# Products of zeros and of the identity ahead of 14 TensorE operations in a fused attention and gating kernel

## The chip, the cores and the metric

The kernel runs on one core of a Trainium2 chip. The metric is the device time of one execution in microseconds (us). Engines are named as in the profile: PE is TensorE's matmul stream and PEld its weight loads, DVE is VectorE, ACT is ScalarE, POOL is GpSimd, SP is SyncE.

## The reference

Two layers are computed one after the other. The first is linear attention with positive random features, for 8 batches, 8 heads, 576 positions and 64 channels; the second mixes along the sequence by a Fourier product and gates the result.

```python
def phi(x):                                    # x: q or k, scaled
    h = x @ omega.T - sum(x * x) / 2           # 128 features
    return exp(h - max(h)) / sqrt(128)
q_p, k_p = phi(q), phi(k)
num = q_p @ (k_p.T @ v)
den = q_p @ sum(k_p) + 1e-6
x = num / den                                  # heads side by side: (8, 576, 512)
x1, x2, x3 = split(x @ w_proj)
y = x1 * irfft(rfft(x2) * rfft(filter_fft)) * x3
out = y @ w_out
```

The kernel does the Fourier transforms as matmuls with tables of sines and cosines that it makes itself at the start.

## The kernel before

Each batch's 576 positions are four tiles of 128 and a rest of 64; the rests of two batches are joined. All matmul operands are bf16.

Per batch, attention does this. **Turns** of keys and queries (`turn_keys`, `turn_queries`, both through `transposes`): eight 128x128 matmuls with the identity `ident` turn a half of `kn` or `qn` into a PSUM bank `h`, and VectorE (ScalarE for later queries) copies it to `kt` or `qt`. **Scores** (`key_features`): eight matmuls of `kt` with the features `om2`, 64 rows each, into a pair of PSUM banks `a`, then one exponential on ScalarE to `ek`; four such units make a batch. There are two pairs `a` and four banks `h`, so a new unit waits until an earlier one has been read. **Values** (`weigh_values`, `max_to_c`): VectorE takes maxima over `ek` (`h<-ek` in the profile, then `mx`), inverts them and scales `vn` to `vc`. **Queries**: 512-column matmuls of `qt` and `om2`, exponential to `eqt`. **Sums**: `ek` times `vc` gives `kv`. **Turn out**: `eqt` times `kv`, divided by VectorE (`xb`), is turned to `xt`. The joined rests go through `left_keys` (`kl`, `klt`, `ekl`, `vcl`) and their own queries. The second layer then projects `xt` with `wproj` (`gates` and `project2`), transforms, multiplies and projects with `wout`.

At the start, VectorE and ScalarE make the tables: `make_residues`, `sines`, then `tables`, which turns them on TensorE into `fwb` and its kin. `half_table` fills `gz`: its upper 64 partitions are zeros, the lower ones a copy of a table.

The order of the work is written out by hand. The kernel's body only records operations: `Plan.record` makes one numbered operation of each call, and joins successive TensorE calls of one stage that write the same PSUM tile into one operation. `ORDER` lists the numbers, and `issue` (line 230, the line of every row in the profile) sends the operations to the engines in that order. Each engine works through its own part in order, and waits between engines follow from the data. Loads are issued from POOL's queue, stores and small moves from SP's.

In the stretch that the prediction speaks of, TensorE's queue runs: first query turns of batch 0, the turn of omega, the rest's key turns, the other query turns, the rest's key scores (`klt`), key turns of batch 0, turns of tables (`gtab`, `xf`), then key scores and key turns of batches 0 and 1 interleaved with queries of batch 0. VectorE copies `kt` four times there, once for each half of the keys of batches 0 and 1.

Of the kernel before, what the change touches and what calls it, by code (L numbers as in the profile page):

```python
# [20 lines left out]

P = 128

CROSSED = {"keys": 5, "queries": 5, "out": 5}

ORDER = """
599 29 33 31 34 56 30 9 0 32 57 3 5 4 38 27 39 28 6 2 40 35 50 49 7 51 52 45 46 55 53 11 12 23 47 41
42 43 71 99 24 48 72 138 8 85 97 44 70 1 26 54 74 73 16 18 13 86 25 87 10 88 37 76 586 64 98 588 589
36 65 100 67 69 58 66 68 600 89 59 90 91 590 75 60 62 61 143 149 92 63 140 93 112 114 150 152 154
155 587 145 14 22 21 111 591 113 151 153 161 101 108 110 156 94 102 107 109 103 104 105 157 163 162  # L30
159 95 106 164 139 158 160 165 96 115 116 126 127 211 120 181 121 128 182 123 229 122 124 125 117 20
144 172 223 118 119 174 175 177 166 230 167 176 135 178 133 593 224 171 247 134 136 131 129 225 173
130 132 227 596 168 169 170 17 19 214 595 603 602 604 179 180 615 617 248 195 196 197 616 146 618
192 193 194 147 231 233 15 78 611 613 249 213 189 217 623 597 250 592 598 190 186 191 625 594 187
188 258 260 624 83 221 286 626 200 201 202 204 203 137 183 185 184 226 321 612 198 205 206 609 199
734 614 228 207 601 661 322 208 610 232 673 662 262 660 81 212 235 236 80 289 670 736 209 290 234
632 251 264 735 257 605 210 259 148 215 77 218 606 674 671 252 667 216 672 237 291 295 668 296 238
293 675 607 292 253 261 347 627 142 737 254 350 676 628 141 255 669 256 294 679 680 284 222 738 687
663 82 348 220 79 263 298 297 740 664 608 665 299 688 629 300 726 677 678 728 239 240 241 242 244
630 243 245 246 265 266 631 666 305 685 686 641 642 643 267 275 633 648 649 650 689 647 652 655 651  # L40
645 276 277 693 694 705 278 691 692 706 634 636 635 656 657 707 653 708 644 709 637 279 306 280 281
282 654 639 646 268 269 307 308 309 270 681 658 659 323 682 310 283 324 365 325 271 366 272 219 303
739 359 304 367 369 371 372 360 319 301 320 741 695 362 342 619 273 690 727 302 700 696 343 697 364
621 373 344 274 823 361 822 729 374 722 723 363 316 724 480 311 620 730 699 701 318 474 725 313 745
315 312 732 747 710 684 683 349 622 345 638 640 702 698 703 746 375 731 749 748 317 314 704 346 713
714 758 326 355 329 742 733 330 743 353 288 287 351 331 760 893 840 895 368 385 370 824 744 386 829
841 711 712 337 451 452 327 376 377 378 328 720 338 750 842 751 719 752 334 335 379 830 285 332 383
384 333 425 476 354 897 848 899 849 356 357 894 755 339 336 394 756 432 757 477 358 434 340 715 896
753 825 387 721 754 905 716 341 832 844 845 388 717 826 827 907 419 481 396 828 428 781 782 783 759
898 900 718 430 762 393 862 833 389 863 856 857 771 917 761 773 390 395 919 831 391 768 769 784 838  # L50
770 839 786 772 427 397 84 843 774 763 775 764 765 767 776 766 381 846 399 847 429 785 834 835 777
778 852 853 431 398 433 836 850 837 851 400 392 380 483 352 787 382 800 801 401 402 788 435 789 790
794 403 404 906 405 908 486 882 411 436 876 489 412 795 877 858 859 491 802 437 438 413 791 780 921
878 879 860 855 864 865 861 406 493 922 803 495 779 439 854 881 407 793 408 440 883 804 414 415 866
416 818 918 488 479 424 923 819 490 475 924 453 454 417 920 870 867 869 871 455 418 874 884 909 911
426 880 891 890 449 820 805 409 821 796 872 450 446 410 469 797 496 448 798 925 868 497 873 470 471
927 885 792 926 928 932 886 892 441 498 443 934 499 887 472 799 910 912 806 888 945 423 422 875 807
947 492 473 442 444 1027 500 501 502 1092 901 903 1094 946 445 485 889 1009 447 902 948 949 904 503
1093 958 494 462 960 959 463 1095 459 942 943 482 961 944 929 930 1014 962 460 950 951 952 464 1015
537 808 1084 1086 931 815 933 465 816 809 810 811 817 1080 1082 505 954 953 466 467 935 484 420 421  # L60
478 936 461 1081 456 457 1012 1013 955 971 973 956 458 507 937 1083 938 468 543 544 957 963 939 545
1010 1011 940 1035 546 1036 913 812 1085 563 915 564 1087 540 539 972 914 984 1028 941 542 813 508
916 1029 1019 487 985 986 541 975 974 1031 509 1020 1032 1051 1104 1106 504 968 1018 510 511 512 513
964 519 521 1052 514 1016 1017 1033 516 969 970 1100 1102 1034 1021 515 518 1105 1101 517 1045 965
506 976 1030 520 1022 1046 522 523 1103 547 1023 548 549 1107 550 524 1025 530 977 978 525 979 980
526 538 1026 1096 1043 1044 1047 1098 1097 1037 1038 1024 1048 527 1049 1088 1090 1050 1099 528 529
531 533 1039 534 967 1005 1006 1112 535 814 1114 532 536 557 554 559 966 996 999 556 1000 1040 551
1053 1089 553 555 558 997 1065 560 1066 1054 1055 1057 1091 1056 1279 565 1113 566 1058 552 1059
1115 998 1042 1001 1041 1215 1061 561 1071 567 562 1069 574 575 576 1070 1063 577 578 1064 1068 1281
981 982 983 1072 990 1132 579 991 992 581 582 1271 1273 583 1060 1197 1280 571 584 1062 1282 1134  # L70
993 572 573 1275 994 585 1120 1277 1116 1117 1118 568 1119 1276 1121 1214 1196 1199 569 1007 1008
995 1272 1067 570 1278 1200 1133 1123 1222 1122 1274 1135 1124 1198 1125 1136 1002 1223 1201 580
1129 1203 1202 1003 1130 1204 1004 1131 1230 1108 987 1231 988 989 1126 1218 1205 1127 1206 1216
1219 1220 1221 1236 1237 1238 1232 1233 1110 1235 1234 1137 1128 1208 1239 1209 1078 1077 1079 1138
1073 1217 1224 1225 1139 1140 1074 1174 1175 1176 1076 1155 1159 1157 1075 1158 1160 1210 1211 1156
1171 1177 1178 1179 1207 1240 1241 1141 1162 1161 1163 1164 1244 1165 1109 1111 1167 1166 1172 1245
# [157 lines left out]
def kernel(  # L234
# [11 lines left out]
    nc = Plan(tc.nc, tc)  # L246
# [29 lines left out]
    def bank():  # L276
        return nc.tile(psum, [P, 512], FP32, name="h", bufs=4)

    def bank_t():
        return nc.tile(psum, [P, 512], FP32, name="h", bufs=4)  # L280
# [42 lines left out]
    ident = nc.tile(const, [P, P], BF16, name="ident")  # L323
# [48 lines left out]
    for j in range(2):  # L372
        nc.vector.tensor_scalar_mul(
            out=om2[j * D : (j + 1) * D, :], in0=omt[:D, :MF], scalar1=qk_scale
# [28 lines left out]
    gz = nc.tile(const, [P, EC], BF16, name="gz")  # L403
# [2 lines left out]
    hps = nc.tile(const, [P, 3, DM], BF16, name="hps")  # L406
    hqs = nc.tile(const, [P, 3, DM], BF16, name="hqs")
    lo64, hi64 = slice(0, 64), slice(64, 128)

    residues = {}  # L410

# [86 lines left out]
            )  # L498

    def half_table():  # L500
        nc.vector.memset(gz[hi64], 0.0)
        nc.vector.tensor_copy(out=gz[lo64], in_=gtab[lo64, 2, HC : HC + EC])
        nc.vector.memset(gtab[lo64, 2, HC : HC + EC], 0.0)

    def tables():
# [3 lines left out]
            out=dup[:, 0], in_=gta[:, SL // 2 : SL // 2 + SL].unsqueeze(1).to_broadcast([P, 2, SL])  # L509
        )  # L510
        nc.vector.tensor_copy(
            out=dup[:, 1:3], in_=gns[:, :, SL // 2 : SL // 2 + SL].unsqueeze(2).to_broadcast([P, 2, 2, SL])
# [4 lines left out]
        dupf = dup[:].rearrange("p c j s -> p c (j s)")  # L517

        ps = bank()
        pb = ps[:].bitcast(BF16).rearrange("p (g c) -> p g c", g=8)  # L520
        for g in range(8):
            m, kt_ = g // 3, g % 3
            nc.tensor.transpose(
                out=pb[:, g],
# [122 lines left out]
    xt_tiles = {}  # L647
    kv_tiles = {}

    def transposes(dst, srcs, scalar=False):  # L650

        ps = bank_t()
        pb = ps[:].bitcast(BF16).rearrange("p (g c) -> p g c", g=8)
        for g, src in enumerate(srcs):
            nc.tensor.transpose(out=pb[:, g, :], in_=src, identity=ident[:])
        if scalar:
            nc.scalar.copy(out=dst, in_=pb[:, 0 : len(srcs)])
        else:
            nc.vector.tensor_copy(out=dst, in_=pb[:, 0 : len(srcs)])
# [34 lines left out]
    def key_features(*units):  # L694

        made = []
        for ek_out, kts in units:
            ps = two_banks()
            made.append(ps)
            for g, kt in enumerate(kts):  # L700
                for j in range(2):
                    nc.tensor.matmul(
                        out=ps[:, j, g * MF : (g + 1) * MF],
                        lhsT=kt[rows[j]],
                        rhs=om2[rows[j]],
                        start=True,
                        stop=True,
                    )
        for ps, (ek_out, _) in zip(made, units):
            nc.scalar.activation(  # L710
                out=ek_out, in_=ps[:].rearrange("p j (g m) -> p j g m", m=MF), func=AF.Exp
            )
# [686 lines left out]
```

## Time and profile before

| | us |
|---|---|
| three executions | 257.41, 258.19, 259.14 |
| their median | 258.19 |
| profiled execution | 259.44 |
| its span in the profile | 257.4 |
| PE busy | 238.1 (92%) |
| DVE busy | 217.9 (85%) |
| ACT busy | 200.7 (78%) |
| POOL busy | 62.6 (24%) |

The profiled execution is one of its own. It is 2.0 us longer than its span, which counts from the first to the last instruction. Busy shares are means over the whole span, and the stages differ: what limits the first 40 us need not be what limits the rest, so views of single stretches are of more use here. In a row of the timeline the first number is the start, the second the duration of the group, then engine, line, operation, output and inputs, form and count; a bracket at the end gives the idle time of the engine just before and what ended it.

### The profile page before, as it was taken

The page shows a single profiled execution, that of the slowest core. Times are in us where ns is not written, and L with a number is a line of the kernel's source. Part 1 is how long each engine was busy: PE and PEld are TensorE (multiplying, and loading weights), DVE is VectorE, ACT ScalarE, POOL GpSimd, SP SyncE. Part 2 cuts the span into 40 slices and gives each one's busy share as a digit, 9 for nine tenths or more (in the row PEclk, how much of TensorE's full clock was granted, in tenths as well). Part 3 has the DMA queues.
Part 4 walks back from the last instruction along what each step waited for, and adds up shares of the span by engine and source line. Part 5 has one row for each costly group of instructions (what it writes and reads, how often), then busy time and mean ns, then how long its engine had stood idle before and what let it go on. Part 6 is the DMA issues. An engine that isn't in the chain of part 4 may idle for free.

```text
span 257.4 us, 5843 instructions
## 1 busy us (share of the span) xinstructions
PE 238.1 (92%) x2282; PEld 139.2 (54%) x2282; DVE 217.9 (85%) x494; ACT 200.7 (78%) x324; POOL 62.6 (24%) x87
## 2 busy tenths in 40 slices
PE   0688699999999999999999979999999999999993
PEld 0555565655667465545566635555555545556641
DVE  6879998589697989999999887999867899899970
ACT  4689398899999999996888847894786568757653
POOL 8456363784007209403037000000000000000000
PEclk9999999999999999999999999999999999999998
DMA  6999999999938999998999977431635524223166
GB/s 83 184 193 178 198 173 140 146 167 176 155 85 128 157 141 110 160 138 142 149 230 128 177 91 188 100 68 34 140 110 143 109 80 122 81 62 113 52 230 220
DMA packets 86787, 35.28 MB, mean 137 GB/s; under 512 B 58219, under 2 KB 81256, under 8 KB 86760
## 3 DMA queue, kind: packets, MB, share of 16 engines
q0 software_dynamic: 59616, 17.31, 65.0%
q1 hardware_dynamic: 27000, 17.47, 27.4%
q8 instruction: 18, 0.29, 0.5%
q10 hardware_dynamic: 144, 0.13, 0.2%
q14 instruction: 9, 0.07, 0.1%
HBM read 34.64 MB, written 9.44 MB: 171 GB/s over the span
## 4 chain that ended last, share of the span: by engine, by line
PE 71%; DVE 10%; DMA 9%; ACT 6%; issue 1%; POOL 1%; SPq 0%; ACTq 0%; DVEq 0%
PE h L230 59%; PE a L230 12%; DMA qn<-in_q_dram 4%; DMA out_dram<-osb 4%; ACT osb L230 2%; DMA sw<-sp 1%; DVE h L230 1%; DVE vc L230 1%; DVE xb L230 1%; DVE kt L230 1%; ACT x L230 1%; DVE xt L230 1%; DVE vcl L230 1%; DVE qt L230 1%; ACT yt L230 1%
## 5 line engine op out<-in xcount | busy, mean ns | idle before, releaser
L230 PE MATMUL h<-xt,wproj 128*128 128x512 bf16 x256 | 64.5, 379 | 1.6 <-ACT osb L230 1.6
L230 ACT CAST x<-h 128x512 bf16<-128x512 f32 x68 | 40.1, 606 | 13.3 <-PE h L230 12.9
L230 PEld LDWEIGHTS <-wproj 128*128 128x128 bf16 x384 | 31.1, 98 | 27.5 <-issue 3.7
L230 ACT ACTIVATE osb<-h 128x512 f32<-128x512 f32 (+4 forms) x49 | 27.2, 566 | 12.5 <-PE h L230 4.1
L230 ACT ACTIVATE eqt<-a 128x1024 bf16<-128x1024 f32 x32 | 32.6, 1048 | 3.4 <-PE a L230 3.1
L230 ACT ACTIVATE ek<-a 128x1024 bf16<-128x1024 f32 x32 | 33.1, 1050 | 1.7 <-PE a L230 1.6
L230 PE MATMUL h<-wproj,xf 128*128 128x512 bf16 x128 | 32.4, 379 | 0.0
L230 PE MATMUL h<-wout,yt 128*128 128x512 bf16 x128 | 31.4, 379 | 0.0
L230 POOL DMA_DIRECT2D qn<-in_q_dram x26 | 23.7, 918 | 20.3 <-DMA qt<-qn 12.6
L230 DVE TENSOR_TENSOR x<-h,x 128x512 bf16<-128x512 f32 x32 | 21.7, 685 | 5.2 <-PE h L230 4.3
L230 PEld LDWEIGHTS <-yt 128*128 128x128 bf16 x128 | 12.1, 98 | 13.8 <-DVE vc L230 0.4
L230 PEld LDWEIGHTS <-xf 128*128 128x128 bf16 x134 | 12.1, 98 | 12.7 <-issue 1.0
L230 PE MATMUL h<-x,fwb 128*128 128x512 bf16 x72 | 18.6, 379 | 0.0
L230 DVE TENSOR_TENSOR xb<-a,rden 128x512 bf16<-128x512 f32 x24 | 16.2, 684 | 0.4
L230 PEld LDWEIGHTS <-eqt 128*128 128x128 bf16 x256 | 11.7, 98 | 6.0 <-DVE xb L230 1.0
L230 PE MATMUL a<-om,kt 64*128 64x128 bf16 x256 | 13.2, 231 | 1.3 <-ACT eqt L230 0.5
L230 PE MATMUL a<-kv,eqt 128*128 128x65 bf16 x256 | 13.0, 194 | 1.5 <-DVE xb L230 0.8
L230 PE MATMUL h<-ident,qn 128*128 128x128 bf16 x80 | 7.2, 238 | 7.4 <-DMA qn<-in_q_dram 7.4
L230 ACT CAST sp<-h 128x512 bf16<-128x512 f32 x16 | 9.7, 603 | 5.6 <-PE h L230 5.5
L230 DVE RECIPROCAL rden<-a 128x8 f32<-128x8 f32 x36 | 7.1, 200 | 7.1 <-PE a L230 6.9
L230 PE MATMUL h<-gtab,xs 128*128 128x193 bf16 x64 | 13.0, 247 | 0.0
L230 PE MATMUL a<-qt,om 64*128 64x512 bf16 x64 | 11.6, 389 | 1.1 <-ACT ek L230 0.3
(164 smaller groups left out, 512.1 us busy)
## 6 DMA issues: line engine op xcount, KB each, us to landing
out_dram<-osb SPq DMA_DIRECT2D x24, 256.0 KB, 2.3
vn<-in_v_dram POOLq DMA_DIRECT2D x8, 512.0 KB, 8.3
kn<-in_k_dram POOLq DMA_DIRECT2D x7, 512.0 KB, 8.6
qn<-in_q_dram POOLq DMA_DIRECT2D x24, 128.0 KB, 8.2
sw<-sp SPq DMA_DIRECT2D x16, 128.0 KB, 2.4
wproj<-in_moe_w_proj_dram POOLq DMA_DIRECT2D x3, 512.0 KB, 8.2
qn<-in_q_dram POOLq DMA_DIRECT2D x2, 512.0 KB, 7.6
out_dram<-xf SPq DMA_DIRECT2D x4, 256.0 KB, 2.9
```

Source lines behind the costliest of these rows:

```text
L230: getattr(real, name)(*args, **kw)
```

## The change

A table `WARM` names, by stage and batch, how many products are put in front of successive operations. `warm` issues them into the PSUM tile that the operation is about to write, with `start=True` each, so that the operation's own first write replaces what they left. For the queries of batch 0 the operands are `gz`'s upper half, 64 rows of zeros by 193 columns, in front of the turn that stands first in TensorE's queue; elsewhere both are the identity, 128 rows by 128 columns. Eight more identity products stand in `tables`. The zeroing of `gz`'s upper half moves from `half_table` to where `gz` is made; it was and is the first instruction of VectorE. `ORDER` is renumbered for that and otherwise lists the same operations in the same order.

```diff
+WARM = {
+    ("turn", "turn queries", 0): [0, 28],
+    ("turn", "keys", 0): [4, 0],
+    ("score", "left keys", 0): [14],
+    ("score", "keys", 0): [4, 4, 4, 3],
+    ("turn", "keys", 1): [4, 4],
+    ("score", "keys", 1): [4, 4, 4, 4],
+}
...
+    nc.vector.memset(gz[hi64], 0.0)
...
     def half_table():
-        nc.vector.memset(gz[hi64], 0.0)
         nc.vector.tensor_copy(out=gz[lo64], in_=gtab[lo64, 2, HC : HC + EC])
...
         ps = bank()
+        for _ in range(8):
+            nc.tensor.matmul(out=ps[:, 0:P], lhsT=ident[:], rhs=ident[:], start=True, stop=True)
         pb = ps[:].bitcast(BF16).rearrange("p (g c) -> p g c", g=8)
...
+    warms = {k: list(v) for k, v in WARM.items()}
+
+    def warm(kind, ps):
+        counts = warms.get((kind, *nc.where))
+        if not counts:
+            return
+        n = counts.pop(0)
+        if kind == "turn" and nc.where[0] == "turn queries":
+            a, w = gz[hi64, 0:P], gz[hi64, :]
+        else:
+            a, w = ident[:], ident[:]
+        for _ in range(n):
+            nc.tensor.matmul(out=ps[:, 0 : w.shape[-1]], lhsT=a, rhs=w, start=True, stop=True)
+
     def transposes(dst, srcs, scalar=False):
 
         ps = bank_t()
+        warm("turn", ps)
...
             ps = two_banks()
             made.append(ps)
+            warm("score", ps[:, 0])
```

The lists are used up from the left in the order of the recorded program. Note two things: the counts follow the program and not `ORDER`, so within the scores of the keys of batch 0 the list reads first unit 4, second 4, third 4, fourth 3, while TensorE's queue takes the unit with 3 first; and the first turn of queries in the program has 0, the second, which is first in the queue, 28.

## The prediction

> **What bounds the kernel now.** I read four views, in this order: the page's engine rows, the windows by stage, the chain of waits in order of time, and the timelines of TensorE and VectorE over the first 37 us. The windows first:
>
> ```profile
> 12.90:21.60 8.70, 7.85 (x83) 5.30 (x84) 6.85 (x19) 7.60 (x9) 5.97 (x8) 1.00 1.51 193
> 21.60:37.00 15.40, 11.61 (x178) 8.26 (x178) 14.98 (x29) 11.28 (x15) 8.66 (x12) 1.00 1.69 182
> 37.00:257.40 220.40, 214.13 (x1986) 122.08 (x1985) 186.56 (x413) 174.65 (x291) 39.64 (x50) 1.00 0.85 132
> 252.70:256.10 3.40, 0.68 (x4) 0.10 (x1) 0.28 (x1) 0.98 (x2) 0.00 (x0) 1.00 0.94 324
> 256.20:257.40 1.20, 0.00 (x0) 0.00 (x0) 0.00 (x0) 0.00 (x0) 0.00 (x0) 0.50 0.00 0
> ```
>
> The columns are length, then busy time of PE, PEld, DVE, ACT, POOL, the clock, DMA. From 37 us on TensorE sets the pace (214 of 220 us, and the chain stays on it nearly throughout). From 21.6 to 37 us VectorE does: 14.98 of 15.40 us, and in that stretch it waits for no other engine. Before 13 us the chain runs through the tables on VectorE and ScalarE, which take nothing late from TensorE. Only between 13 and 21.6 us does VectorE wait for TensorE. The waits of VectorE in that window are one line, and its timeline shows the three places:
>
> ```profile
> DVE kt L230 <- PE h L230: 1.8, 3, 0.8
> ```
>
> ```profile
> 15.37 0.69 DVE L230 COPY kt<-h 128x1024 bf16<-128x1024 bf16 x1 [0.62 <-PE h L230]
> ...
> 18.60 0.69 DVE L230 COPY kt<-h 128x1024 bf16<-128x1024 bf16 x1 [0.82 <-PE h L230]
> 19.21 0.28 DVE L230 COPY xf<-gns 128x256 bf16<-128x256 bf16 x1
> 19.34 1.22 DVE L230 TENSOR_TENSOR h<-ek 128x2048 bf16<-128x2048 bf16 x1
> 20.87 0.69 DVE L230 COPY kt<-h 128x1024 bf16<-128x1024 bf16 x1 [0.31 <-PE h L230]
> ```
>
> So 1.76 us (0.62 + 0.82 + 0.31) is all that a faster TensorE can take out of the path. ScalarE sits beside it: its exponentials run almost without a break from 13.27 us, when its table is loaded, to 26.8 us, with 0.48 and 0.38 us lost to TensorE in this window.
>
> **The clock.** The page's clock digit is 9 from the first slice, because the trace records only changes: the first record is at 20.6 us. What stood before it is read from TensorE's own timeline:
>
> ```profile
> 7.20 1.03 PE L230 MATMUL h<-ident,qn 128*128 128x128 bf16 x8 [7.20 <-DMA qn<-in_q_dram]
> ...
> 13.00 0.29 PE L230 MATMUL h<-ident,xf 128*128 128x128 bf16 x1 [0.20 <-DVE mk L230]
> ...
> 18.50 0.61 PE L230 MATMUL a<-qt,om 64*128 64x512 bf16 x2
> ...
> 20.77 0.39 PE L230 MATMUL a<-qt,om 64*128 64x512 bf16 x2
> ...
> 21.59 0.40 PE L230 MATMUL a<-om,kt 64*128 64x128 bf16 x8
> 21.92 0.62 PE L230 MATMUL h<-ident,qn 128*128 128x128 bf16 x8
> 22.47 0.39 PE L230 MATMUL a<-qt,om 64*128 64x512 bf16 x2
> ```
>
> The same pair of 512-column products takes 0.61 us at 18.50 and 0.39 us at 20.77; eight turns take 1.03 us before and 0.62 us after. TensorE is at half clock until 20.6 us. One turn costs (1.03 - 0.29)/7 = 0.106 us at half clock; at full clock eight turns hold the next operation back 0.55 us (21.92 to 22.47) and eight scores 0.33 us (21.59 to 21.92), against 0.96 and 0.54 us before.
>
> [...]
>
> [...]
>
> **The change part by part.** All other engines keep their instructions and their order; TensorE gets 93 products.
> - **28 zero products before the first turn of queries.** Zeros are written on VectorE at 0.85 to 1.07 us, already first in its queue, so nothing is pushed back. By columns one takes 193/128 x 0.106 = 0.16 us, 28 take 4.5 us: from 1.1 to 5.6 us at half clock, and less if it opens on the way. The first turn waits for its data until 7.20 us. Cost nothing, with 1.6 us to spare. [...] No row shows zeros; from below they count as nothing (the clock then opens by about 10 to 14 us, from turns and fills), from above as any product; I take the latter, since the row nearest is any matmul of the same shape.
> - **Staying open.** Between 5.6 and 7.2 us TensorE is idle. [...]
> - **14 identity products before the scores of the left keys.** 14 x 0.057 = 0.8 us, laid from about 9.3 us; these scores wait for VectorE's om2 until 11.01. Nothing at full clock, 0.2 us at half.
> - **8 before the tables' turns and 3 before the first scores.** They lie before a wait for VectorE's xf (12.95) and kt (13.61 us). Nothing at full clock.
> - **The other 40,** four before each of ten operations, 0.23 us a time. Before the scores whose keys VectorE has yet to copy they lie in a wait; before the three turns of keys (one of batch 0, two of batch 1) and before the second and fourth scores of batch 0 they stand in the queue and delay.
>
> **The sum.** First scores from 13.75 us (kt sets it). Then 0.33 of scores, 0.23 of fills, 0.62 of turns: kt copied at 14.97 instead of 15.37. Second scores: 0.55 + 0.23 + 0.40 after 14.31, ScalarE at 15.53 instead of 15.91. Third and fourth exponentials follow at ScalarE's 0.92 us: 16.45 and 17.36, each 0.38 early. The fourth scores' fills wait for the bank that the second exponential frees at 16.6; then 0.23, 0.33, 0.23 and 0.62 to the end of the next turns: 18.01, kt at 18.05 instead of 18.60, 0.55 early. h<-ek follows at 18.79 (the fourth exponential is done at 18.4) and leaves VectorE at 19.93; the last turns: scores start at 18.79 behind kt, 0.33, 0.23, 0.62, end at 19.97; kt at 20.01 instead of 20.87. **0.86 us early.** From there VectorE is its own bound to 37 us: ScalarE's last exponential comes 0.6 us early, still ahead of its reader at 27.4 - 0.86; v of batch 0 landed at 19.5 us against a use at 25.1, q of batch 1 at 16.5 against 21.9, the projection weights for the gates at 34.6 against 39.6. So the start of TensorE's full stretch moves by the same 0.86 us, and its work beyond is unchanged, as the last fill lies before 25 us.
>
> The profiled execution took 259.44 us (span 257.4): 258.6 after. The median of the runs is 258.19, 1.25 us below it; taking 0.86 off that gives **257.3 us**.
>
> **Rivals.**
> - **The clock falls back, or opens late** (near 12 to 14 us): the first two steps are lost, fills at half clock take some of the rest; gain about 0.3 us, 257.9. [...]
> - **The runs shown opened earlier than the profiled one.** [...] For it: the profiled time is the longest of the four.
> - [...]
> - **Slower: fills that run at half clock.** If zeros and identity do not open the clock before 20 us, five groups of four lie on the path (one turn and two scores of batch 0, two turns of batch 1) at 0.43 us each, 2.2 us, and 14 and 8 add up to 0.6: 260.4 to 261.0. It decides if the clock is still at half beyond about 13 us. [...]
>
> **How the numbers follow.** Forecast 0.52, fall-back 0.12, earlier runs 0.14, the large gain 0.14, slower 0.08. The likeliest alone: 256.6 to 257.9. The range reaches to the large gain below and past the small ones above: 255.8 to 259.0. About 1% (2.6 us) is what a measurement of this kernel can tell from no change; the sum caps near 1.8 us, so faster by over 1% takes the large gain with its late phases, and some scatter: 0.2; slower by over 1% the cold fills at their worst: 0.07.
>
> **What would show it.** Right: zero products at 1.1 us, eight query turns at 7.2 us taking 0.62 us, a clock record between 3.5 and 7 us; VectorE's waits for PE h at kt between 13 and 21 us at 0.9 instead of 1.8 us; PE's full stretch from 36.4. Wrong: turns at 1.03 us beyond 10 us, a second clock record before 20 us, or VectorE waiting anew after 21 us.

## The result and the profile after

| | median, us | range of 20 runs |
|---|---|---|
| before | 258.69 | 257.41 to 259.64 |
| after | 256.79 | 256.17 to 258.82 |

The ratio on record is 0.9946, 95% interval 0.9927 to 0.9964, so 1.40 us less (0.93 to 1.89). It equals 256.79 over 258.19, the median of the three executions given before; the medians of this table lie 1.90 us apart. 256.79 us is inside the range of the forecast (255.8 to 259.0, with 257.3 as its number) and within 1% of no change; the 0.86 us of the sum lies just under the interval.

The profiled execution of the changed kernel took 258.82 us (span 256.9) and is the slowest of its twenty. Its TensorE waited for the load of the rest's keys (`kl`) until 9.75 us where a second execution turns them from 8.58 us, and that delayed what hangs on it. So I read two executions: this one for the clock, the second (the first run below, 256.11 us) for the sum. TensorE's timeline of the first, in pieces:

```profile
1.13 4.71 PE L239 MATMUL h<-gz 64*128 64x193 bf16 x28 [1.13 <-DVE gz L239]
7.24 1.04 PE L239 MATMUL h<-ident,qn 128*128 128x128 bf16 x8 [1.41 <-DMA qn<-in_q_dram]
9.75 0.58 PE L239 MATMUL h<-ident,kl 128*128 128x128 bf16 x4 [1.22 <-DMA kl<-in_k_dram]
...
10.98 1.70 PE L239 MATMUL a<-ident 128*128 128x128 bf16 x14
...
13.15 1.03 PE L239 MATMUL h<-ident,kn 128*128 128x128 bf16 x8
...
15.92 0.61 PE L239 MATMUL h<-ident,kn 128*128 128x128 bf16 x8
```

The zeros stand where they were meant to, at 1.13 us, and end at 5.8. The first turns still take 1.04 us, so **the zeros have not opened the clock**. The 14 identity products after the late `kl` hold the left keys' scores back, and the key turns of 13.15 still run at half clock; those of 15.92 take 0.61 us. The first clock record is at 14.43 us (20.61 before). The row of VectorE's waits between 12.9 and 21.6 us:

```profile
DVE kt L239 <- PE h L239: 2.6, 3, 1.2
```

In this execution they are longer than before's 1.8 us. The windows, columns as before:

```profile
36.00:256.90 220.90, 215.71 (x2007) 123.31 (x2004) 188.45 (x415) 176.34 (x294) 41.17 (x52) 1.00 0.87 133
```

TensorE is busy for 215.7 of the 220.9 us from 36 us to the end. VectorE's scaling `vc<-vn` of the second batch, which marks the start of that stretch, begins at 36.82 us, 0.8 us later than before's 36.00; and yet the execution is 0.6 us shorter. So two things had to be told apart: what the start gives, and what is gained beyond it.

### The profile page after: what moved, and what is told of

Same layout as the page of the kernel before. It is cut to its first block, busy times and chain, and to the rows that moved or that the text cites. A ratio compares the mean times of both kernels' runs of the same rounds, so it can differ in the third digit from the quotient of the medians.

```text
span 256.9 us, 6029 instructions
## 1 busy us (share of the span) xinstructions
PE 244.4 (95%) x2375; PEld 145.8 (57%) x2375; DVE 218.0 (85%) x494; ACT 200.7 (78%) x324; POOL 62.6 (24%) x87
## 4 chain that ended last, share of the span: by engine, by line
PE 76%; DVE 8%; DMA 7%; ACT 4%; SPq 1%; issue 1%; POOL 1%; ACTq 0%; POOLq 0%; DVEq 0%
PE h L239 63%; PE a L239 13%; DMA out_dram<-osb 4%; DMA kl<-in_k_dram 2%; ACT osb L239 2%; DVE h L239 2%; DMA sw<-sp 1%; DVE xb L239 1%; DVE vc L239 1%; SPq L239 1%; DVE kt L239 1%; DVE vcl L239 1%; ACT sp L239 1%; DVE mx L239 1%; DVE qt L239 0%
## 5 line engine op out<-in xcount | busy, mean ns | idle before, releaser
L239 PEld LDWEIGHTS <-yt 128*128 128x128 bf16 x128 | 12.1, 98 | 13.8 <-DVE vc L239 0.4
L239 PE MATMUL a<-om,kt 64*128 64x128 bf16 x256 | 12.2, 218 | 0.5 <-DVE xb L239 0.4
L239 PEld LDWEIGHTS <-fwb 128*128 128x128 bf16 x81 | 7.4, 98 | 7.7 <-issue 0.2
```

The source lines that it names most:

```text
L239: getattr(real, name)(*args, **kw)
```

## The experiments

In each heading the ratio is against the kernel before on the same chip, with its 95% interval. "Start" is the begin of the second batch's `vc<-vn` on VectorE; "after the start" is the span less that. A run has one profiled execution, and it need not be like the median one; where the two differ, the text says so.

### The changed kernel again: 0.9914 (0.9889 to 0.9940)

No edit. 256.28 us, against 258.55 before on this chip.

> The changed kernel itself, unedited, for a second execution in the profile. Theory A (the zero products do not open the clock; the 65 identity products do, at about 10.5 to 14.5 us): turns of queries at 7.2 us take 1.03 us, the first clock record lies between 10 and 15 us; with the loads of kl landed near 8.1 us as before, VectorE's waits for kt between 12.9 and 21.6 us are 0.9 to 1.4 us. Rival B (the zeros open the clock in most grids and the profiled execution was an exception): first clock record between 3.5 and 7 us, turns at 7.2 us 0.62 us. Time 256.8 us, ratio 0.993 to 0.996 by either.

"Grids" in rival B stands for executions that differ in when the clock opens (16.58 to 22.92 us in the profiles of kernels without fills).

Its rows of TensorE, of VectorE and of VectorE's waits:

```profile
7.37 1.04 PE L239 MATMUL h<-ident,qn 128*128 128x128 bf16 x8 [1.54 <-DMA qn<-in_q_dram]
...
9.84 1.20 PE L239 MATMUL a<-ident 128*128 128x128 bf16 x14
...
11.35 0.62 PE L239 MATMUL h<-ident,kn 128*128 128x128 bf16 x8
```

```profile
14.88 0.69 DVE L239 COPY kt<-h 128x1024 bf16<-128x1024 bf16 x1
...
18.03 0.69 DVE L239 COPY kt<-h 128x1024 bf16<-128x1024 bf16 x1 [0.75 <-PE h L239]
18.77 1.22 DVE L239 TENSOR_TENSOR h<-ek 128x2048 bf16<-128x2048 bf16 x1
19.99 0.69 DVE L239 COPY kt<-h 128x1024 bf16<-128x1024 bf16 x1
```

```profile
DVE kt L239 <- PE h L239: 0.7, 1, 0.7
```

The turns of 7.37 run at half clock here too. The clock opens at 10.35 us, inside the 14 fills (1.20 us instead of 1.70), and the key turns of 11.35 take 0.62 us. The copies `kt` start at 14.88, 18.03 and 19.99 us; the sum said 14.97, 18.05 and 20.01. One wait of 0.7 us is left of 1.8. The start is 35.12 us, **0.88 early where 0.86 was forecast**. After the start 219.0 us are left, against 221.4 in the profile of before: another 2.4 us, which the forecast did not have.

### Without the 28 zeros: 0.9916 (0.9888 to 0.9944)

```diff
-    ("turn", "turn queries", 0): [0, 28],
+    ("turn", "turn queries", 0): [0, 0],
```

> The 28 zero products are left out, the 65 identity products stay. A: the zeros did nothing, so the time is that of the changed kernel, 256.8 us, ratio 0.994 within 0.002, clock record between 10 and 15 us. B: the clock opens 4 to 7 us later than with zeros, the first scores and turns run slow, 257.4 us, ratio about 0.997.

256.16 us, beside 256.28 with them. The first clock record is at 11.59 us, the start again at 35.12. The zeros are worth nothing.

### The zeros alone: 0.9991 (0.9969 to 1.0013)

All lists but that of the queries are set to zeros, and the loop of 8 in `tables` to `range(0)`.

> Only the 28 zero products stay; the 65 identity products are left out. A: as the kernel before, ratio 0.998 to 1.001, clock record near 14 to 21 us. B: clock record between 3.5 and 7 us if it does not fall back, ratio 0.993 or better, as the identity products no longer stand in TensorE's queue.

258.51 us beside 258.55: the kernel before. TensorE's row with the zeros is the same to the digit, and the key turns that took 0.62 us in the run above are at half clock:

```profile
1.13 4.71 PE L239 MATMUL h<-gz 64*128 64x193 bf16 x28 [1.13 <-DVE gz L239]
...
11.56 1.03 PE L239 MATMUL h<-ident,kn 128*128 128x128 bf16 x8
```

```profile
DVE kt L239 <- PE h L239: 1.8, 3, 0.8
```

The first clock record is at 20.65 us. **The whole gain belongs to the 65 identity products**: 2.2 us between this run and the first, on one chip. Their two profiled executions lie 2.5 us apart: the start gives 0.91 of that (36.03 to 35.12) and what follows 1.6 (220.6 to 219.0).

### Whole numbers in place of the zeros: 0.9916 (0.9892 to 0.9940)

Are zeros too poor in data to count? 24 products on 128 rows of the table `si` take the place of the 28.

```diff
-    ("turn", "turn queries", 0): [0, 28],
+    ("turn", "turn queries", 0): [0, 24],
...
-            a, w = gz[hi64, 0:P], gz[hi64, :]
+            a, w = si[:, 0:64].bitcast(BF16), si[:, 100:196].bitcast(BF16)
```

> The 28 zero products are replaced by 24 products of the same length on 128 rows of the table of whole numbers that POOL makes at 2.5 to 2.9 us (data that is not zero), the identity products stay. [...] B (zeros count like any product): the same time as the changed kernel within 0.1%.

256.36 us, within 0.1% of the changed kernel, as B has it; the first clock record is at 12.23 us. Still it does not show that zeros count: these 24 products did not open the clock before 12.23 us either, though their data is not zero and fills 128 rows. `si` is ready later than `gz`; whether that is the reason was not shown.

### Zeros in place of the identity: 0.9931 (0.9907 to 0.9955)

```diff
-            a, w = ident[:], ident[:]
+            a, w = eql_buf[0][:, 0, 0, :], eql_buf[0][:, 0, 0, :]
```

`eql_buf` holds zeros on 128 rows at that time. The 8 in `tables` become 64-row zeros of `gz`.

> The 65 identity products become products of zeros in the same places (57 of 128 rows from a tile that is zero until 47 us, the 8 of the tables of 64 rows); the 28 zeros at the start stay. Theory A (only products of data that is not zero open the clock): the clock record comes no earlier than in the kernel before, near 14 to 21 us or later, and the products now stand in TensorE's queue at half clock: 0.4 us each time four stand on the path, so slower than before, 259 to 261 us, ratio 1.001 to 1.010. Rival B (any product counts, and the zeros at the start were lost only to their 64 rows): clock record at 10 to 14.5 us, 256.3 us, ratio 0.992.

256.80 us, 0.7% below before on its chip. TensorE:

```profile
9.99 1.70 PE L239 MATMUL a<-eql 128*128 128x128 bf16 x14
...
12.16 0.68 PE L239 MATMUL h<-ident,kn 128*128 128x128 bf16 x8
```

The 14 fills of zeros end at 11.7 us, the clock opens at 12.32, and the turns of 12.16 are the first that run mostly at full clock. Without any fill of 128 rows (the run before the last) it stayed at half until 20.65. So zeros count, and what set the 28 apart was not their data. They differ in two other things: they fill 64 rows of the array and not 128, and they stand earlier, before 5.9 us.

### Only the first 25 fills: 0.9959 (0.9929 to 0.9989)

14, 8 and 3 stay; the zeros and the other 40 go.

```diff
-    ("score", "keys", 0): [4, 4, 4, 3],
-    ("turn", "keys", 1): [4, 4],
-    ("score", "keys", 1): [4, 4, 4, 4],
+    ("score", "keys", 0): [0, 0, 0, 3],
+    ("turn", "keys", 1): [0, 0],
+    ("score", "keys", 1): [0, 0, 0, 0],
```

> Only the first 25 identity products stay (14 before the left keys' scores, 8 in the tables, 3 before the first scores); no zeros, none of the other 40. If those 25 open the clock and it stays open by the kernel's own work, the 40 were on the path for nothing: VectorE's third wait for kt shrinks from 0.75 to 0.3 us or less, time 0.3 to 0.45 us below the changed kernel: 255.9 us, ratio 0.990. [...]

VectorE has the `kt` copies without a bracket, so without a wait:

```profile
17.17 0.69 DVE L239 COPY kt<-h 128x1024 bf16<-128x1024 bf16 x1
...
19.13 0.68 DVE L239 COPY kt<-h 128x1024 bf16<-128x1024 bf16 x1
```

The start is 34.26 us, 1.74 early: the whole 1.76 us of the three waits. The 40 fills thus cost 0.86 us of start (34.26 against 35.12). But the time is 257.53 us where 255.9 was expected: worse than with them (256.28) and with more scatter (256.56 to 259.61). After the start 221.2 us are left, about as before the change. In the waits from 36 us to the end stands one that the first run does not have:

```profile
PE h L239 <- ACT osb L239: 2.0, 1, 2.0
```

A second thing stands in the record of the single executions. The mean granted clock is 0.993 or less in 4 of these 12; they took 258.98 us in the median, the other eight 257.21. The mean leaves out the time up to the first clock record (the profile of before has 0.997, with half clock until 20.6 us), so a low mean says that the clock was at half again later: by estimate 0.993 is 3.6 us at half clock, and in the profiles the end of the run accounts for 1.4 us at most. Such a mean is seen in 58 of 140 executions of the kernels without the 40 later fills (before among them), in 2 of the 6 with whole numbers, and in none of the 61 of the other kernels with all 65 fills. So the 40 go with a clock that stays open. No execution with such a mean was profiled; where its clock fell, and whether near the start, is not shown.

### Where the rest is: a store near 150 us

That wait is in the profile of before too: TensorE's timeline, then ScalarE's.

```profile
151.47 1.03 PE L230 MATMUL h<-xt,wproj 128*128 128x512 bf16 x4
...
154.12 1.02 PE L230 MATMUL h<-xt,wproj 128*128 128x512 bf16 x4 [1.63 <-ACT osb L230]
```

```profile
153.47 1.09 ACT L230 ACTIVATE osb<-h 128x512 f32<-128x512 f32 x2 [3.14 <-DMA out_dram<-osb]
```

TensorE waits 1.63 us for a bank that ScalarE empties into `osb`; ScalarE waits 3.14 us for a buffer `osb`, which a store issued at 144.28 us still holds 9 us later, as the chain of waits has it:

```profile
144.28 9.11 DMA out_dram<-osb
```

In the first run the two rows are

```profile
150.35 1.89 PE L239 MATMUL h<-xt,wproj 128*128 128x512 bf16 x8
```

```profile
150.55 0.60 ACT L239 ACTIVATE osb<-h 128x512 f32<-128x512 f32 x1 [0.81 <-PE h L239]
```

where the eight matmuls follow each other without a break and ScalarE waits for TensorE, not for the store. Just before it, from 133 to 139 us, POOL's queue issues loads of `q` of batches 6 and 7 and `v` of batch 7. The small load `vl` behind them took 13.8 us from issue to landing before, and 8.9 us in the first run:

```profile
DMA to landing us min/median/max: 13.8/13.8/13.8
```

```profile
DMA to landing us min/median/max: 8.9/8.9/8.9
```

What stands directly ahead of the store in SP's own queue is not one of these loads. From batch 5 on the kernel turns keys and queries by transposing moves (DMA transfers that transpose on the way), and one of them is issued 3.0 us before the store (1.6 us in the first run):

```profile
141.24 2.94 SPq L230 DMA_TRANSPOSE kt<-kn  x1
```

```profile
140.12 1.46 SPq L239 DMA_TRANSPOSE kt<-kn  x1
```

By the completion signals in the traces this move ends at 151.65 us before and at 148.52 in the first run, the store at 153.39 and 149.06. In all fourteen traces the store ends 0.5 to 1.8 us after the move. So the store comes in right behind a move that itself takes 10.4 and 8.4 us here.

Two readings were open. Either any gain at the start reaches this store and is carried or lost there; or something else about the kernel decides it. The next two runs move the arrival by other means.

### Before, with four matmuls less after the start: 1.0001 (0.9964 to 1.0038)

Four of the eight 512-column products of the first gates are left out near 40 us.

```diff
+                    n_ct = (1 if off == 0 else 3) if (b, nb) == (0, 0) else CB
-                    for ct in range(CB):
+                    for ct in range(n_ct):
```

> The kernel before, with 4 of the 8 matmuls of 512 columns of one product of the first gates left out (near 40 and 46 us; part of x1 and x3 of batch 0 is not computed): TensorE's full stretch is 4 x 0.216 = 0.86 us shorter there, as if it had begun 0.86 us earlier; the clock at the start is as before. Theory T (the second half of the gain, some 1.3 us beyond 122 us, comes of the earlier timing alone: the store of a result lands in time for its buffer): 256.4 us, ratio 0.992. Rival U (it comes of something else than the timing): only the 0.86 us, 257.7 us, ratio 0.9967, with TensorE idle 1.4 us near 150 us as before.

258.32 us, which neither reading has: no gain from 0.86 us of work less. TensorE still waits 1.2 us for `osb`. In its profile the clock opened only at 22.92 us and the start was 36.37, which eats part of what was taken out.

### After, with four matmuls more after the start: 0.9987 (0.9957 to 1.0017)

```diff
+                    for _ in range(4 if (b, nb, off) == (0, 0, 0) else 0):
+                        nc.tensor.matmul(out=pp[:], lhsT=wproj[:, 0, 0:P],
+                                         rhs=xt_tiles[b][:, 0, 0:SM], start=True, stop=True)
```

> The changed kernel with 4 more matmuls of 512 columns near 41 us in TensorE's full stretch: what the start gained, 0.86 us, is given back there. T: the wait near 150 us returns, ratio 1.000, 258.5 us. U: only the 0.86 us is lost, 257.2 us, ratio 0.995, no wait of TensorE near 150 us.

257.94 us. The nearest kernel on this chip, the one with zero fills (start 35.50), took 256.80: 1.1 us for 0.86 us of work. The profile has the start at 35.12 us and a wait of 0.5 us for `osb`, where the second execution of the changed kernel has none. So the added work and a part of the wait are both paid, which lies between T and U.

### The burst lightened: before, after and the first 25

The load of `v` of batch 7 is left out of three kernels; it is the largest of the burst, 512 KB. Of each the edit is

```diff
+        if (which, b) == ("v", 7):
+            nat_tiles[which, b] = nat_tiles[which, 5]
+            return
```

with `ORDER` renumbered for the missing operation; `v` of batch 5 is read in its place.

> The kernel before without the load of v of batch 7 (512 KB of the burst of loads from 133 to 139 us; v of batch 5 is read in its place, so the output of batch 7 is another). Theory T (near 150 us TensorE waits because a store lands late behind that burst; the changed kernel mostly escapes it): the wait of 1.2 to 1.6 us is gone, time 1.0 to 1.6 us below the kernel before, ratio 0.994 to 0.996. Rival U (the wait has another cause): ratio 0.999 to 1.001.

> The changed kernel without the load of v of batch 7. T: it had nearly no wait to lose, so it gains 0 to 0.4 us on itself and stands 0.86 us below the kernel before without that load: ratio 0.990 to 0.993. U: as the changed kernel, and further than 0.86 us below the kernel before without that load.

> Only the first 25 identity products, without the load of v of batch 7. Its start came 1.74 us early against 0.87 of the changed kernel, and the wait near 150 us took 2.0 us of it. T: without the burst the whole 1.74 us shows: 0.87 us below the changed kernel without that load, ratio 0.986 to 0.989. U: no better than it.

| without that load | us | ratio to before | start, us | after the start, us |
|---|---|---|---|---|
| before | 256.71 | 0.9918 (0.9891 to 0.9945) | 35.05 | 219.5 |
| after | 256.57 | 0.9923 (0.9895 to 0.9951) | 35.12 | 219.4 |
| first 25 | 256.11 | 0.9901 (0.9869 to 0.9933) | 34.59 | 218.8 |

None has a wait for `osb` near 150 us. In before without the load, `vl` lands in

```profile
DMA to landing us min/median/max: 6.1/6.1/6.1
```

where 13.8 us stood before, and the transposing move ends 5.2 us after its issue instead of 10.4 (4.7 and 5.3 us in the other two). All three have some 219 us after the start. **The wait goes with the burst of loads**, and the kernel before gains 2.3 us (258.99 to 256.71) when it is lightened, more than the 1.0 to 1.6 that were expected. The first 25 lie 0.46 us below after, where 0.87 was expected; two of their six executions have a mean clock of 0.983 and 0.987. What was not expected is that before and after are then equal. A part of the answer is in the profile of before without the load, in VectorE's waits and TensorE's timeline:

```profile
DVE kt L230 <- PE h L230: 0.8, 2, 0.6
```

```profile
16.12 0.60 PE L230 MATMUL a<-om,kt 64*128 64x128 bf16 x8 [0.25 <-DVE kt L230]
16.99 0.40 PE L230 MATMUL a<-om,kt 64*128 64x128 bf16 x8 [0.27 <-ACT ek L230]
```

Scores take 0.60 us at 16.12 and 0.40 us at 16.99: with no fill at all, the clock of this execution opened at 16.58 us, not at 20.61 as in the profile of before, and the waits shrank by themselves from 1.8 to 0.8 us. One profile can't say how often that happens. The ten runs (255.56 to 258.02) spread over 2.5 us, the six with the fills (256.23 to 257.13) over 0.9.

### Zeros on 128 rows at the start, no identity: 0.9967 (0.9936 to 0.9997)

```diff
-            a, w = gz[hi64, 0:P], gz[hi64, :]
+            z = eql_buf[0][:].rearrange("p a h c -> p (a h c)")
+            a, w = z[:, 0:P], z[:, 0:EC]
```

24 of them, and all 65 identity products out.

> 24 products of zeros on all 128 rows (193 columns) from 3.4 us on in place of the 28 on 64 rows, and none of the 65 identity products. [...] Rival S (zeros count only beside other data): clock record at 14 to 21 us, ratio 0.999 to 1.001.

```profile
3.42 4.06 PE L239 MATMUL h<-eql 128*128 128x193 bf16 x24 [3.42 <-DVE zb L239]
7.33 1.03 PE L239 MATMUL h<-ident,qn 128*128 128x128 bf16 x8
...
9.74 0.61 PE L239 MATMUL h<-ident,qn 128*128 128x128 bf16 x8
```

The same kind of product as the 28, on twice the rows, opens the clock at 8.78 us; the zeros and the turns behind them keep TensorE busy from 3.42 to 8.61 us. The record at 14 to 21 us that rival S has did not come. The start is 34.25 us, as with the first 25 fills, with nothing left to pay on the path. The wait of TensorE for `osb` is there (1.1 us), and 220.1 us are left after the start. This profiled execution took 256.41 us, no more than the changed kernel; the median is 257.82. Nine of the twelve executions have a mean clock of 0.972 to 0.993, and they took 258.26 in the median against 256.41 of the three others. So, by the same reading, the clock fell back in most of them: it opened early in the profile, and stayed open only in some executions.

## Why the prediction was right, and where not

- **The start: right.** Fills open the clock, VectorE's waits for `kt` shrink from 1.8 to 0.7 us (0.9 forecast), and the three copies came within 0.1 us of their worked-out times. 0.88 us measured in the second execution, 0.86 forecast. The price of the 40 later fills at the start was in the sum rightly too: 0.90 us there (1.76 less 0.86), 0.86 us by the run without them. (The sign "full stretch from 36.4" does not follow from the sum: 37.0 less 0.86 is 36.1.) The cap of 1.76 us was right as well: 1.74 and 1.75 in the two runs without these 40.
- **"From above as any product; I take the latter": the step that failed,** with no effect on the time. In the profile of the changed kernel the 64-row zeros run from 1.13 to 5.84 us without a break and did not open the clock: the turns of 7.24 us take 1.04 us. In three other executions with these zeros the turns of 7.27 to 7.52 us take 1.03 to 1.04 us. So the signs that were named (turns of 0.62 us at 7.2, a record between 3.5 and 7) did not come. No run shows the opening ahead of the first turns that the forecast took; the earliest in a profile is at 8.78 us, with zeros on 128 rows. The record came at 10.3 to 12.5 us in most profiles with the 14 fills, from turns and these. That is the bound "from below" of the same step, whose consequence for the sum I worked out only for a late opening near 12 to 14 us: VectorE first waits for TensorE after 13 us, so an opening before that costs nothing. That the miss cost nothing is luck.
- **"Staying open": not put to the test by the changed kernel,** as its clock opened only after the gap of 5.6 to 7.2 us. That the clock stays open over such a gap was not shown. Zeros on 128 rows opened it at 8.78 us; in the profile it stayed at full over idle times of TensorE of 0.66 us before 11.01 us and 0.93 us before 13.01 us (eight turns take 0.62 us at 11.34 and at 13.99), but nine of twelve executions have a mean clock that speaks of a fall.
- **"14 fills: nothing at full clock, 0.2 us at half": the size depends on `kl`.** In the profiled execution of after, where `kl` came late, they took 1.70 us, and scores forecast from 11.01 us began at 12.61. There the start was 0.8 us late and not 0.86 early. This is the slower rival in small, in the slowest of twenty runs.
- **"Its work beyond is unchanged": failed as to time.** The work is the same, but TensorE's wait near 150 us is 1.1 to 2.0 us in the five profiles with the full burst and without the 40 later products (before, zeros only, before with less, first 25, zeros on 128 rows). In the six with all 65 (or zeros in their place) it is 0 in four, 0.3 in after and 0.5 with the added work. Take this wait off, and what is left after the start lies between 218.8 and 219.8 us in all twelve profiles whose TensorE work there is unchanged. So by the profiles most of what was gained beyond 0.86 us is this wait: 1.63 of the 2.4 us between before and the first run, with 0.8 left without a name. The measured gain is 1.40 us by the ratio (1.90 by the medians) over twenty runs and 2.2 us on the first chip; how the medians divide between the wait and a clock that falls back (six of the nineteen executions of before there have a low mean) is not shown.
- **What stays open** is why the 40 products go with a store that is on time. It isn't the earliness of the start alone: starts 1.74 us early have the wait, starts 0.5 to 0.9 early (without the added work) have none, starts unchanged have it, and a start 0.8 late has 0.3 us of it. With the full burst the transposing move ahead of the store took 8.3 to 11.6 us, and what sets that within this range was not shown, nor what in those products decides it. Shown is that the wait goes with the burst and that the store follows the move.
- **The rival "runs shown opened earlier" is a real case.** The clock of kernels without fills opened at 16.58 to 22.92 us in their profiles, with starts from 35.05 to 36.37. With all 65 it opened at 10.35 to 12.32 us and starts were 35.12 to 35.50, apart from the profile of after with its late `kl` (14.43 and 36.82). So a part of what fills bring is that the executions differ less: the six runs of the changed kernel on the first chip lie within 0.8 us, the nineteen of before within 2.3 us.
- **The large gain of the chances (0.14),** with all three waits closed, did occur at the start in two runs, and yet their medians, 257.53 and 257.82 us, lie above the forecast of 257.3, since the wait near 150 us took back 2.0 and 1.1 us of it in the profiles, and the mean clock is low in 4 and 9 of their twelve executions: the places were right, the arithmetic "start gained is time gained" was not. No run shows what its "late phases" are worth; the latest opening in a profile is at 22.92 us, without fills, with a start 0.37 us later than in before.

## What to carry to other kernels

The products with which the clock opened early here were on 128 rows: the 14 of the identity or of zeros behind the first turns (10.35 to 12.32 us, or 14.43 with `kl` late), or 24 of zeros ahead of them (8.78 us). Put such products where their engine waits for others anyhow. After the opening each further one on the path is paid (0.86 us of start for 40 here), and yet the kernel without these 40 was the slower one, so judge them by many executions and their mean clock, not by one profile. Work out where the gain is consumed before adding such products: only 1.76 us of VectorE's waits stood behind 7.6 us at half clock (13 to 20.6). And when the measured gain is larger than the sum, compare the waits far from the change: here a store behind a transposing move and a burst of loads, 110 us later, made TensorE wait 0 to 2.0 us in kernels that differ only in the start, and a lighter burst took the wait away without the change.

## What the runs showed of the hardware

- **Zeros count, and rows may.** With zeros on 128 rows in place of the identity the clock opened at 12.32 us, with 24 of them ahead of the first turns at 8.78 us, and with the 28 zeros on 64 rows alone not before 20.65 us. Those 28 take 4.71 us and left the first turns at 1.03 to 1.04 us in four profiles. The rival is time: those zeros end at 5.84 us, and no profile shows an opening before 8.78 us. Rows alone do not settle it either: 24 products of whole numbers on 128 rows ahead of the same turns did not open the clock before 12.23 us.
- **When the clock opened, and when it fell.** Without fills it opened at 16.58 to 22.92 us in the profiles, with the kernel's own work alone ahead of it, and with the 64-row zeros alone at 20.65 us. In before it fell at 256.13 us, with 0.68 us of TensorE's work between 252.7 and 256.1 us. How much work opens the clock, and how little keeps it, was not shown.
- **A store can take 9 us behind a transposing move beside a burst.** Stores from SP's queue take 2.8 us in the median between 130 and 156 us of the kernel before; the one issued at 144.28 us, behind a transposing move in the same queue and amid 1.4 MB of loads from POOL's queue, freed its buffer only at 153.4, 1.7 us after the move ended. With 512 KB less in the burst the move took 4.7 to 5.3 us instead of 8.3 to 11.6.
